# A third pair of F tiles by seven block products, with loads, block sums and the units' order moved to suit, in a SwiGLU kernel on one core

## The chip, the cores and the metric

The kernel runs on one core of one Trainium2 chip. The metric is the device time of one execution in microseconds (us); from several runs the median is given. Engines are named as in the profile: PE is TensorE, ACT ScalarE, DVE VectorE, POOL GpSimd, SP SyncE, which issues most transfers.

## The reference

```python
B, S, D, F = 1, 2048, 512, 1376          # all bfloat16
def reference(x, w_gate, w_up, w_down):
    g = jax.nn.silu(x @ w_gate)          # [2048, 1376]
    u = x @ w_up
    return (g * u) @ w_down              # [2048, 512]
```

## The kernel before

**Tiling.** The 2048 tokens are four chunks of 512 (`SC`); chunks 0 and 1 are the first half (`pi = 0`), 2 and 3 the second (`pi = 1`). F is ten tiles of 128 and a remainder of 96. The ten tiles form five pairs; pair `u` holds tiles `2u` and `2u+1`. `xT_sb` holds x transposed (D on the partitions), `w_sb` gate and up weights, `wd_sb` w_down. `h0_sb` and `h1_sb` hold h = silu(gate) * up for the two token halves.

**Two ways to make h.** A *classic* tile (F tile, chunk) is 4 matmuls for gate and 4 for up in bfloat16 (`gu_emit` at L410, each split in two column halves, or `gu_whole` at L421), then a silu on ACT and a product on DVE (`classic_out`). A *unit* (token half, pair) treats two F tiles x two chunks x two halves of D as a 2x2 block product and makes it with seven block products instead of eight, for gate and for up: `p1` and `p2` in bfloat16 (L605), and `p6`, `p5`, `p7`, `p3`, `p4` (L593) with 4-byte operands that are sums of blocks. A unit has 28 matmuls, four classic tiles have 32. The sums of weight blocks S1 to S4 and a cast A22 are made by `w_sums` in `ss_sb` (POOL, casts on ACT or POOL; four slots); the sums of token blocks T1 to T4 and a cast B22 by `x_sums` in `tt_sb` (DVE for the first half, POOL for the second). S2 reads S1, S4 reads S2; T2 reads T1, T4 reads T2. Products after p7 and p3 leave through adds on DVE (`sums`, into `ts_sb`), a silu on ACT and a product on POOL; those after p2 and p4 through a silu and a DVE product (`direct`). `p1` and `keep` copy partial sums aside on ACT and DVE.

`U_ORDER` says which pairs are units in which half: before, pairs 3 and 4 of the first half and all five of the second. The other tiles of the first half are classic.

**Order.** TensorE's order is the order in which the program calls these functions; SP's is that of the `load` calls. ACT, DVE and POOL get theirs from `Plan.schedule`, a list planner: it repeatedly takes the operation that could start first by its model (busy and lag of each operation, landing times of the loads), and among equal starts the one with the lower `prio`. `after` adds dependences. Planned times set only the order; at run time semaphores decide.

TensorE's order before: transposes of the first 256 tokens, classic tiles 0 and 1 of chunk 0, classic tiles 2 to 5 of chunk 0, classic tiles 0 to 2 of chunk 1, the remainder of F for all four chunks (`plan_x`, `plan_y`, L474 and L500, which need x2 and x3), p1 of the first unit, then the units. One classic tile of chunk 1 stands ahead of the first unit's p6, one between its p6 and p5, and one in the last unit ahead of p3. In each unit the order is p6, p5, p7, p2, p1 of the next unit, p3, p4. The weight sums of pair 0 are made first; DVE's `x_sums(0)` waits for them (`after`), the weight sums of the first half's pairs wait for `x_sums(0)`, and `x_sums(1)` on POOL waits for these.

After the units comes the down product (`down`): matmuls over h for half of the tokens' tiles, the remainder's (`tails`), and `DownUnit`, again with seven block products, whose sums DVE and POOL make (`down_sums`; T1 and T2 in `tt_sb`, T3 and T4 in `th_sb`, which lies over `w_sb`). POOL gets the h products of the units at priority 3, weight sums at 8.

SP's loads before: `xn` (first 256 tokens), gate and up weights of tiles 0-1 (`wg0`, `wu0`) with `x0b` between them, tiles 2-3 (`wg2`, `wu2`), tiles 4-5 (`wg4`, `wu4`), `x1`, tiles 6-7, tiles 8 and on, `wut`, `x2`, `x3`, then w_down. x beyond the first 256 tokens comes by transposing transfers.

Of the kernel before, what the change touches and what calls it, by code (L numbers as in the profile page):

```python
# [5 lines left out]
ALU = mybir.AluOpType  # L6
BF16 = mybir.dt.bfloat16
FP32 = mybir.dt.float32
# [6 lines left out]
A_BUSY, A_LAG = 485, 180  # L15
# [152 lines left out]
def bass_standalone__swiglu_ffn__prompt_kernel(nc, x, w_gate, w_up, w_down, out):  # L168
    _, S, D = x.shape
    F = w_gate.shape[1]  # L170
    P = 128
    KD = D // P
    KH = KD // 2
    NFF = F // P
    U_ORDER = [[3, 4], [0, 3, 4, 1, 2]]
    F_LAST = F - NFF * P
    SC = 512
    NSC = S // SC
# [13 lines left out]
    xf = x[0]  # L192
# [5 lines left out]
    with ExitStack() as es:  # L198
# [25 lines left out]
        ss_sb = sb("ss_sb", [P, NSLOT, 5, 2, KH, P], F32R)  # L224
        tt_sb = [tt0_sb, sb("tt1_sb", [P, 5, KH, SC], F32R)]
# [24 lines left out]
        plan = Plan()  # L250
        engines = {"P": nc.tensor, "S": nc.sync, "A": nc.scalar, "D": nc.vector, "G": nc.gpsimd}

        landed = 2700

        def load(name, emit, writes, busy, lag):
            nonlocal landed
            landed += lag
            i = take(homes[name] if name in homes else rest[0])
            plan.add("S", emit, writes=writes, busy=busy, lag=1800, dma=(i, 16)).land = landed + (2500 if landed > 10000 else 0)

        slabs = [(0, 2), (2, 4), (4, 6), (6, 8), (8, NFF + 1)]
        slab_of = {ft: a for a, b in slabs for ft in range(a, b)}

        def load_w(name, src, m, c0, f0, f1):
            load(
                name,
                lambda e: e.dma_start(  # L267
                    w_sb[:, :, m, c0:c0 + f1 - f0], src[:, f0:f1].rearrange("(k p) f -> p k f", p=P)
                ),
                [name], 600, 3.2 * (f1 - f0),  # L270
            )

        def load_slab(a, b):
            load_w(f"wg{a}", w_gate, 0, a * P, a * P, min(b * P, F))
            load_w(f"wu{a}", w_up, 1, a * P, a * P, min(b * P, F - 32))

        def load_x(name, t0, t1):
            load(
                name, lambda e: e.dma_start_transpose(xT_sb[:, :, t0:t1], xf[t0:t1, :]), [name], 1500, 4.6 * (t1 - t0)  # L279
            )  # L280

        load(
# [6 lines left out]
        load_w("wg0", w_gate, 0, 0, 0, slabs[0][1] * P)  # L289
        load_x("x0b", HT, SC)  # L290
        load_w("wu0", w_up, 1, 0, 0, slabs[0][1] * P)
        for a, b in slabs[1:3]:
            load_slab(a, b)
        load_x("x1", SC, 2 * SC)
        for a, b in slabs[3:]:
            load_slab(a, b)
        load_w("wut", w_up, 0, F, F - 32, F)
        for c in range(2, NSC):
            load_x(f"x{c}", c * SC, (c + 1) * SC)
        load(  # L300
            "wd",
            lambda e: e.dma_start(
# [31 lines left out]
        def tt_op(engs, out, a, b, alu, reads, writes, prio, busy, after=()):  # L334
            return plan.add(
                engs, lambda e: e.tensor_tensor(out, a, b, alu), reads, writes, busy,  # L336
                G_LAG if engs == "G" else D_LAG, prio, after=after,
            )
# [44 lines left out]
        for dk in range(KD):  # L383
            keys = [("b", 2 * dk), ("b", 2 * dk + 1)] if dk < KD - 1 else [("b", 6)]
# [136 lines left out]
        W_SUM = {"S1": 0, "S2": 1, "S3": 2, "S4": 3, "A22": 4}  # L521
        X_SUM = {"T1": 0, "T2": 1, "T3": 2, "B22": 3, "T4": 4}
        slot_of = {}

        def cast_op(eng, out, src, reads, writes, prio, busy, after):
            plan.add(
                eng, lambda e: e.activation(out, src, ACT.Copy) if eng == "A" else e.tensor_copy(out, src),
                reads, writes, busy, A_LAG if eng == "A" else G_LAG, prio, after=after,
            )

        def w_sums(u, prio, after, casts):

            f0, f1 = 2 * u * P, (2 * u + 1) * P
            slot = len(slot_of) % NSLOT
            slot_of[u] = slot
            block = lambda m, k, f: w_sb[:, k * KH:(k + 1) * KH, m, f:f + P]
            at = lambda n, m: ss_sb[:, slot, W_SUM[n], m, :, :]
            key = lambda n, m: ("ss", slot, n, m)
            wkey = lambda m: f"w{'gu'[m]}{slab_of[2 * u]}"
            for n in ("S1", "S2", "S3", "S4"):  # L540
                for m in range(2):
                    A11, A12, A21, A22 = (block(m, k, f) for f in (f0, f1) for k in range(2))
                    rd = lambda n: at(n, m).bitcast(FP32)
                    a, b, alu, of_ = {
                        "S1": (A21, A22, ALU.add, ()), "S2": (rd("S1"), A11, ALU.subtract, ["S1"]),
                        "S3": (A11, A21, ALU.subtract, ()), "S4": (A12, rd("S2"), ALU.subtract, ["S2"]),
                    }[n]
                    last = tt_op(
                        "G", at(n, m), a, b, alu, [wkey(m)] + [key(o, m) for o in of_], [key(n, m)], prio, 640, after
                    )  # L550
            for m in range(2):
                cast_op(casts, at("A22", m), block(m, 1, f1), [wkey(m)], [key("A22", m)], prio, 360, after if casts == "G" else ())
            return [last]

        def x_sums(pi, eng, prio, after):

            c0, c1 = 2 * pi, 2 * pi + 1
            xk = x_keys(c0) + x_keys(c1)
            key = lambda n, k: ("tt", pi, X_SUM[n], k)
            steps = [(0, KH)] if eng == "D" else [(k, k + 1) for k in range(KH)]  # L560
            for n in ("T1", "T2", "T3", "T4"):
                for k0, k1 in steps:
                    block = lambda k, c: xT_sb[:, k * KH + k0:k * KH + k1, c * SC:(c + 1) * SC]
                    at = lambda n: tt_sb[pi][:, X_SUM[n], k0:k1, :]
                    rd = lambda n: at(n).bitcast(FP32)
                    B11, B12, B21, B22 = (block(k, c) for k in range(2) for c in (c0, c1))
                    a, b, of_ = {
                        "T1": (B12, B11, ()), "T2": (B22, rd("T1"), ["T1"]),
                        "T3": (B22, B12, ()), "T4": (B21, rd("T2"), ["T2"]),
                    }[n]  # L570
                    last = tt_op(
                        eng, at(n), a, b, ALU.subtract, xk + [key(o, k) for o in of_ for k in range(k0, k1)],
                        [key(n, k) for k in range(k0, k1)], prio, 1150 if eng == "D" else 1250, after,
                    )
            for k in range(KH):
                cast_op("A", tt_sb[pi][:, X_SUM["B22"], k, :], xT_sb[:, KH + k, c1 * SC:(c1 + 1) * SC], xk, [key("B22", k)], prio, A_BUSY, ())
            return [last]

        class Unit:
            def __init__(self, pi, u, banks):  # L580
# [90 lines left out]
        wkey = [f"wg{slab_of[0]}", f"wu{slab_of[0]}"]  # L671
# [320 lines left out]
        units = [(pi, u) for pi in range(2) for u in U_ORDER[pi]]  # L992
        early = [2 * u + i for u in range(NFF // 2) if u not in U_ORDER[0] for i in range(2)]
        sums = w_sums(0, 8, (), "A")
        for fts in [[2, 3]] + [[ft] for ft in early[4:]]:
            classic(0, fts)
        for ft in early[:-3]:
            classic(1, [ft])
        sums = x_sums(0, "D", 6, sums)
        for u in U_ORDER[0]:  # L1000
            sums = w_sums(u, 8, sums, "A")
        sums = x_sums(1, "G", 8, sums)

        pool_last = []

# [67 lines left out]
```

## Time and profile before

| | |
|---|---|
| runs shown | 115.79, 116.16, 117.97 us; median 116.16 |
| profiled execution | 115.73 us, span 114.4 us, clock 1.00 |
| busy, share of the span | PE 96%, PEld 58%, DVE 67%, ACT 53%, POOL 52% |
| chain that ended last | PE 91%, DMA 3%, SP's queue 2% |
| seven-block matmuls of the units | 140, busy 35.3 us |
| units, up to the down product | 26.04 to 75.69 us |

Times in the profile run from the start of the span. The chain lists, back from the last instruction, what released each step; a stretch of it on one engine is a stretch in which only that engine's work set the end.

### The profile page before, as it was taken

Reading aid. Unit: us, or ns where it says so; the run is one execution under the profiler, and the core shown is the slowest. Engines: PE = TensorE matmul, PEld = TensorE weight load, DVE = VectorE, ACT = ScalarE, POOL = GpSimd, SP = SyncE. Lnnn points to the kernel's source line nnn. Section 1 sums busy time; section 2 is a strip of 40 time slices with the busy share of each in tenths; the row PEclk is TensorE's granted clock in tenths of the full one; section 3 lists DMA queues with packets and bytes.
Section 4 is the critical chain, followed back from the end, with each engine's and each line's share of the span. In section 5 each row is a group of like instructions: output and inputs, shape, how many; then the busy total and the mean of one; then the engine's idle time right before and its main releaser. Section 6 shows DMA issues by size and latency. Waiting matters only on the chain.

```text
span 114.4 us, 1807 instructions
## 1 busy us (share of the span) xinstructions
PE 110.3 (96%) x662; PEld 66.7 (58%) x670; DVE 76.3 (67%) x112; ACT 60.9 (53%) x116; POOL 59.9 (52%) x75
## 2 busy tenths in 40 slices
PE   7989999999999999999999999999999999999993
PEld 2645555554567667685858677554344657866452
DVE  0112599766659395776849393799999987486423
ACT  5344285599756767878676767630576960000000
POOL 1475000599999999799999999981000000000000
DMA  3999999993000000000000000000041002327966
GB/s 96 255 307 257 212 282 232 239 356 78 0 0 0 0 3 3 0 6 0 3 0 0 0 0 0 0 6 0 2 135 46 0 0 46 52 46 183 200 190 207
DMA packets 22776, 9.84 MB, mean 86 GB/s; under 512 B 12816, under 2 KB 22640, under 8 KB 22768
## 3 DMA queue, kind: packets, MB, share of 16 engines
q1 hardware_dynamic: 20624, 8.69, 31.1%
q10 hardware_dynamic: 2144, 1.05, 3.2%
q8 instruction: 5, 0.08, 0.3%
q14 instruction: 3, 0.02, 0.1%
HBM read 4.75 MB, written 2.10 MB: 60 GB/s over the span
## 4 chain that ended last, share of the span: by engine, by line
PE 91%; DMA 3%; SPq 2%; issue 1%; DVE 1%
PE psum L593 28%; PE psum L703 15%; PE psum L410 12%; PE psum L605 10%; PE psum L841 10%; PE psum L421 5%; PE psum L853 4%; DMA w_sb<-in_w_up_dram 3%; PE psum L474 3%; PE psum L731 3%; PE psum L500 2%; SPq L279 1%; DVE o_sb L325 1%; SPq L267 0%; SPq L284 0%
## 5 line engine op out<-in xcount | busy, mean ns | idle before, releaser
L593 PE MATMUL psum<-tt_sb,ss_sb 128*128 128x512 f32 x140 | 35.3, 404 | 0.0
L593 PEld LDWEIGHTS psum<-tt_sb,ss_sb 128*128 128x128 f32 x140 | 26.3, 188 | 6.4
L336 DVE TENSOR_TENSOR ts_sb<-r_sb,psum 128x512 f32<-128x512 f32 x28 | 17.9, 682 | 12.4 <-ACT r_sb L324 12.4
L336 DVE TENSOR_TENSOR h_sb<-sg_sb,psum 128x512 bf16<-128x512 f32 x26 | 17.8, 683 | 8.6 <-PE psum L410 7.0
L331 ACT ACTIVATE sg_sb<-psum 128x512 f32<-128x512 f32 x26 | 15.5, 598 | 14.5 <-PE psum L410 8.0
L336 POOL TENSOR_TENSOR ss_sb<-w_sb 128x256 fp32r<-128x256 bf16 x20 | 13.1, 677 | 15.1 <-DVE tt_sb L336 11.1
L336 POOL TENSOR_TENSOR h_sb<-sg_sb,ts_sb 128x512 bf16<-128x512 f32 x14 | 18.4, 1316 | 1.7 <-ACT sg_sb L331 1.5
L324 ACT ACTIVATE r_sb<-psum 128x512 f32<-128x512 f32 x28 | 15.2, 595 | 5.7 <-PE psum L593 5.7
L703 PE MATMUL psum<-wd_sb,h_sb 128*128 128x512 bf16 (+2 forms) x97 | 18.0, 335 | 0.2
L410 PE MATMUL psum<-xT_sb,w_sb 128*64 128x512 bf16 (+1 forms) x160 | 15.9, 358 | 0.7 <-DMA w_sb<-in_w_up_dram 0.5
L703 PEld LDWEIGHTS psum<-wd_sb,h_sb 128*128 128x128 bf16 x100 | 8.3, 98 | 9.2 <-issue 1.0
L410 PEld LDWEIGHTS psum<-xT_sb,w_sb 128*64 128x64 bf16 x160 | 8.8, 110 | 7.6 <-DMA w_sb<-in_w_up_dram 0.8
L605 PE MATMUL psum<-xT_sb,w_sb 128*128 128x512 bf16 x52 | 12.6, 380 | 0.4 <-issue 0.2
L331 ACT ACTIVATE sg_sb<-ts_sb 128x512 f32<-128x512 f32 x14 | 8.9, 633 | 1.6 <-DVE ts_sb L336 1.6
L605 PEld LDWEIGHTS psum<-xT_sb,w_sb 128*128 128x128 bf16 x56 | 4.8, 98 | 7.0 <-issue 2.3
L336 POOL TENSOR_TENSOR ss_sb<-w_sb,ss_sb 128x256 fp32r<-128x256 bf16 x10 | 6.6, 686 | 0.0
L336 POOL TENSOR_TENSOR ss_sb<-ss_sb,w_sb 128x256 fp32r<-128x256 f32 x10 | 6.6, 678 | 0.0
L325 DVE CAST o_sb<-psum 128x512 bf16<-128x512 f32 (+2 forms) x6 | 2.9, 512 | 4.2 <-PE psum L703 3.1
L421 PE MATMUL psum<-xT_sb,w_sb 128*128 128x512 bf16 x24 | 5.7, 379 | 0.0
L841 PE MATMUL psum<-tt_sb,ss_sb 128*128 128x512 f32 x20 | 5.7, 420 | 0.0
L324 ACT ACTIVATE o_sb<-psum 128x512 bf16<-128x512 f32 x4 | 2.3, 596 | 6.1 <-PE psum L731 5.1
L325 DVE COPY psum<-psum 128x512 f32<-128x512 f32 x7 | 4.9, 700 | 0.9 <-ACT sgy_sb L331 0.3
(71 smaller groups left out, 126.9 us busy)
## 6 DMA issues: line engine op xcount, KB each, us to landing
wd_sb<-in_w_down_dram SPq DMA_DIRECT2D x1, 1280.0 KB, 7.8
w_sb<-in_w_gate_dram SPq DMA_DIRECT2D x4, 256.0 KB, 4.1
w_sb<-in_w_up_dram SPq DMA_DIRECT2D x4, 256.0 KB, 4.3
out_dram<-o_sb SPq DMA_DIRECT2D x7, 128.0 KB, 1.8
out_dram<-xT_sb ACTq DMA_DIRECT2D x4, 128.0 KB, 2.4
out_dram<-xT_sb ACTq DMA_DIRECT2D x2, 256.0 KB, 3.3
w_sb<-in_w_gate_dram SPq DMA_DIRECT2D x1, 352.0 KB, 4.9
w_sb<-in_w_up_dram SPq DMA_DIRECT2D x1, 320.0 KB, 4.2
```

The costliest lines, as they stand in the source:

```text
L324: return e.activation(out, src, ACT.Copy)
L325: return e.tensor_copy(out, src)
L331: "A", lambda e: e.activation(out, src, ACT.Silu), reads, writes, busy, A_LAG, prio
L336: engs, lambda e: e.tensor_tensor(out, a, b, alu), reads, writes, busy,
L410: ins = e.matmul(psum[h:h + HC, b, n0:n1], lhsT=w_sb[:, dk, m, ft * P + h:ft * P + h + HC], rhs=xT_sb[:, dk, c * SC + n0:c * SC + n1], sta ...
L421: ins = e.matmul(bank(b), lhsT=w_sb[:, dk, m, ft * P:(ft + 1) * P], rhs=xT_sb[:, dk, c * SC:(c + 1) * SC], start=(dk == 0), stop=(dk == KD ...
L474: ins = e.matmul(psum[m:m + HC, b, :], lhsT=w_sb[:, dk, 0, XC0 + m:XC0 + m + HC], rhs=xT_sb[:, dk, c * SC:(c + 1) * SC], start=(dk == 0), ...
L593: ins = e.matmul(bank(dst), lhsT=s[:, k, :], rhs=t[:, k, :], start=(start and k == 0), stop=(k == KH - 1), skip_group_check=True,)
L605: ins = e.matmul(bank(dst), lhsT=w_sb[:, k0 + k, m, f:f + P], rhs=xT_sb[:, k0 + k, c:c + SC], start=(start and k == 0), stop=(k == KH - 1) ...
L703: ins = e.matmul(psum[:, b, 0:c1 - c0], lhsT=hrows(F_ORDER[n], t, 0, P), rhs=wd_sb[:, F_ORDER[n], c0:c1], start=(start and n == n0), stop= ...
L841: ins = e.matmul(bank(dst), lhsT=self.ds[s][:, j, self.q, :], rhs=self.dt[t][:, j, :], start=(start and n == 0), stop=(n == NFF // 2 - 1), ...
L853: ins = e.matmul(bank(dst), lhsT=wd_sb[:, 2 * j + a, d * P:(d + 1) * P], rhs=h0_sb[:, 2 * j + a, 0:SC], start=(n == 0), stop=(n == NFF // ...
```

## The change

1. `U_ORDER` becomes `[[2, 4, 3], [0, 2, 4, 3, 1]]`: pair 2 (tiles 4 and 5) of the first half is a unit too. Classic tiles 4 and 5 of chunks 0 and 1 are gone; so are the classic tiles between p6 and p5 of the first unit and in the last unit.
2. Load order: `x1` directly after tiles 2-3; tiles 6-7 after `x3`. The planner's landing times are set anew.
3. `w_sums` makes each sum for gate and up in one POOL instruction of 512 elements instead of two of 256, which waits for both weights; its A22 casts get priority 8.
4. `x_sums` chains each T after the one before it; its casts get priority 8. Priorities of the later weight sums and of `x_sums(1)` go from 8 to 2.
5. In the last unit p4 comes ahead of p3.

```diff
-    U_ORDER = [[3, 4], [0, 3, 4, 1, 2]]
+    U_ORDER = [[2, 4, 3], [0, 2, 4, 3, 1]]
...
-        for a, b in slabs[1:3]:
-            load_slab(a, b)
+        load_slab(*slabs[1])
         load_x("x1", SC, 2 * SC)
-        for a, b in slabs[3:]:
-            load_slab(a, b)
+        load_slab(*slabs[2])
+        load_slab(*slabs[4])
         load_w("wut", w_up, 0, F, F - 32, F)
         for c in range(2, NSC):
             load_x(f"x{c}", c * SC, (c + 1) * SC)
+        load_slab(*slabs[3])
...
+            block = lambda k, f: w_sb[:, k * KH:(k + 1) * KH, :, f:f + P].rearrange("p k m c -> p m k c")
+            at = lambda n: ss_sb[:, slot, W_SUM[n], :, :, :]
...
             for n in ("S1", "S2", "S3", "S4"):
-                for m in range(2):
...
-                        "G", at(n, m), a, b, alu, [wkey(m)] + [key(o, m) for o in of_], [key(n, m)], prio, 640, after
+                last = tt_op("G", at(n), a, b, alu, wkeys + [k for o in of_ for k in keys(o)], keys(n), prio, 1180, after)
...
+            last = after
             for n in ("T1", "T2", "T3", "T4"):
-                for k0, k1 in steps:
+                before = last
+                last = []
+                for k0, k1 in [(0, KH)] if pi == 0 else [(k, k + 1) for k in range(KH)]:
...
-                        [key(n, k) for k in range(k0, k1)], prio, 1150 if eng == "D" else 1250, after,
+                        [key(n, k) for k in range(k0, k1)], prio, 1160 if eng == "D" else 1250, before,
...
-        for fts in [[2, 3]] + [[ft] for ft in early[4:]]:
-            classic(0, fts)
-        for ft in early[:-3]:
+        classic(0, [2, 3])
+        for ft in early[:3]:
             classic(1, [ft])
         sums = x_sums(0, "D", 6, sums)
         for u in U_ORDER[0]:
-            sums = w_sums(u, 8, sums, "A")
-        sums = x_sums(1, "G", 8, sums)
+            sums = w_sums(u, 2, sums, "A")
+        sums = x_sums(1, "G", 2, sums)
...
-        classic(1, early[-3:-2], [6, 7])
+        classic(1, early[3:], [6, 7])
         for n in range(len(units)):
             unit.p6()
-            if n == 0:
-                classic(1, early[-2:-1], [2, 3])
             unit.p5()
             unit.p7()
             unit.p2()
             if n + 1 < len(units):
                 after = make(n + 1)
                 after.p1()
+                unit.p3()
+                unit.p4()
             else:
-                free = 2 * (1 - n % 2)
-                classic(1, early[-1:], [free, free + 1])
-            unit.p3()
-            unit.p4()
+                unit.p4()
+                unit.p3()
```

More of the change, by code (lines that the diff above doesn't have):

```diff
@@ L258, in load @@
             i = take(homes[name] if name in homes else rest[0])
-            plan.add("S", emit, writes=writes, busy=busy, lag=1800, dma=(i, 16)).land = landed + (2500 if landed > 10000 else 0)
+            plan.add("S", emit, writes=writes, busy=busy, lag=1800, dma=(i, 16)).land = landed + (0 if landed < 5000 else 500 if landed < 10000 else 500)
         slabs = [(0, 2), (2, 4), (4, 6), (6, 8), (8, NFF + 1)]
@@ L269, in load_w @@
                 ),
-                [name], 600, 3.2 * (f1 - f0),
+                [name], 600, 3.7 * (f1 - f0),
             )
@@ L278, in load_x @@
             load(
-                name, lambda e: e.dma_start_transpose(xT_sb[:, :, t0:t1], xf[t0:t1, :]), [name], 1500, 4.6 * (t1 - t0)
+                name, lambda e: e.dma_start_transpose(xT_sb[:, :, t0:t1], xf[t0:t1, :]), [name], 1500, 5.2 * (t1 - t0)
             )
@@ L535, in w_sums @@
             slot_of[u] = slot
[L536 to L539, printed above, removed]
+            block = lambda k, f: w_sb[:, k * KH:(k + 1) * KH, :, f:f + P].rearrange("p k m c -> p m k c")
+            at = lambda n: ss_sb[:, slot, W_SUM[n], :, :, :]
+            keys = lambda n: [("ss", slot, n, m) for m in range(2)]
+            wkeys = [f"w{g}{slab_of[2 * u]}" for g in "gu"]
             for n in ("S1", "S2", "S3", "S4"):
-                for m in range(2):
[L542 to L548, printed above, removed]
-                        "G", at(n, m), a, b, alu, [wkey(m)] + [key(o, m) for o in of_], [key(n, m)], prio, 640, after
-                    )
+                A11, A12, A21, A22 = (block(k, f) for f in (f0, f1) for k in range(2))
+                rd = lambda n: at(n).bitcast(FP32)
+                a, b, alu, of_ = {
+                    "S1": (A21, A22, ALU.add, ()), "S2": (rd("S1"), A11, ALU.subtract, ["S1"]),
+                    "S3": (A11, A21, ALU.subtract, ()), "S4": (A12, rd("S2"), ALU.subtract, ["S2"]),
+                }[n]
+                last = tt_op("G", at(n), a, b, alu, wkeys + [k for o in of_ for k in keys(o)], keys(n), prio, 1180, after)
             for m in range(2):
-                cast_op(casts, at("A22", m), block(m, 1, f1), [wkey(m)], [key("A22", m)], prio, 360, after if casts == "G" else ())
+                cast_op(
+                    casts, at("A22")[:, m], w_sb[:, KH:2 * KH, m, f1:f1 + P], [wkeys[m]], [("ss", slot, "A22", m)], 8, 360,
+                    after if casts == "G" else (),
+                )
             return [last]
@@ L559, in x_sums @@
             key = lambda n, k: ("tt", pi, X_SUM[n], k)
-            steps = [(0, KH)] if eng == "D" else [(k, k + 1) for k in range(KH)]
+            last = after
             for n in ("T1", "T2", "T3", "T4"):
-                for k0, k1 in steps:
+                before = last
+                last = []
+                for k0, k1 in [(0, KH)] if pi == 0 else [(k, k + 1) for k in range(KH)]:
                     block = lambda k, c: xT_sb[:, k * KH + k0:k * KH + k1, c * SC:(c + 1) * SC]
@@ L570, in x_sums @@
                     }[n]
-                    last = tt_op(
+                    last.append(tt_op(
                         eng, at(n), a, b, ALU.subtract, xk + [key(o, k) for o in of_ for k in range(k0, k1)],
-                        [key(n, k) for k in range(k0, k1)], prio, 1150 if eng == "D" else 1250, after,
-                    )
+                        [key(n, k) for k in range(k0, k1)], prio, 1160 if eng == "D" else 1250, before,
+                    ))
             for k in range(KH):
-                cast_op("A", tt_sb[pi][:, X_SUM["B22"], k, :], xT_sb[:, KH + k, c1 * SC:(c1 + 1) * SC], xk, [key("B22", k)], prio, A_BUSY, ())
-            return [last]
+                cast_op("A", tt_sb[pi][:, X_SUM["B22"], k, :], xT_sb[:, KH + k, c1 * SC:(c1 + 1) * SC], xk, [key("B22", k)], 8, A_BUSY, ())
+            return last
         class Unit:
```

## The prediction

> **What bounds the kernel now.** I read the page first (span, busy slices, chain), then the chain of waits in order of time, then the timelines of the engines that feed TensorE, and last the issues and landings of the loads.
>
> ```profile
> span 114.4 us, 1807 instructions
> ...
> PE   7989999999999999999999999999999999999993
> ...
> POOL 1475000599999999799999999981000000000000
> ...
> PE 91%; DMA 3%; SPq 2%; issue 1%; DVE 1%
> ...
> 35.01:75.69 40.68, 40.48 (x178) 28.44 (x181) 28.28 (x46) 28.98 (x56) 39.24 (x42) 1.00 0.01 1
> ```
>
> The last row is from the table of stages (stage, its length, then busy time of PE, PEld, DVE, ACT, POOL, then the granted clock). TensorE (PE) is 91% of the chain, and in the stage of the seven-block units (35.01 to 75.69) it is busy 40.48 of 40.68 us at clock 1.00: there is next to no hole to close. GpSimd (POOL) is busy 39.24 of the same 40.68 us. So time can be won only by taking matmuls away, and lost by making TensorE wait; the engine nearest to making it wait is GpSimd. The chain, piece by piece (start, length):
>
> ```profile
> 6.85 14.00 PE psum L410 x128
> ...
> 23.45 1.73 PE psum L474 x16
> ...
> 26.04 0.16 issue
> 26.20 0.81 PE psum L605 x3
> 27.01 1.73 PE psum L421 x8
> 28.73 0.92 PE psum L593 x4
> 29.65 1.74 PE psum L421 x8
> ...
> 35.01 4.66 PE psum L593 x20
> ...
> 41.41 4.61 PE psum L593 x20
> 46.02 1.74 PE psum L605 x8
> ...
> 72.10 1.73 PE psum L421 x8
> 73.83 1.86 PE psum L593 x8
> ```
>
> From 6.85 us TensorE runs on without a wait: 16 classic groups (14.00/16 = 0.875 us each), the tails (20.85 to 26.04; the row at 23.45 is the product of x2 and then that of x3), the first unit's p1, classic tiles at L421 (1.74 us for gate and up), and units of 20 four-byte matmuls (4.61) and 8 two-byte ones (1.74), 6.35 us a unit.
>
> **The change, part by part.**
>
> *Matmuls.* Pair 2 (F tiles 4 and 5) of chunks 0 and 1 leaves the classic path: four L410 groups, 4 x 0.875 = 3.50 us, and two L421 tiles, 1.73 + 1.74 = 3.47. A unit is added: 4.61 + 1.74 = 6.35. Net -0.62 us, all on the path. This is the whole possible gain: 0.5% of the time.
>
> *What the classic work covered.* 3.50 us of it stood before the tails, 1.74 between p6 and p5 of the first unit, 1.73 in the last unit. Whatever these hid now comes due earlier. The rest asks, for each, what is late next.
>
> *Loads.* The rows give the issue on SP (start, length), and for the loads the time from issue to landing.
>
> ```profile
> 4.20 0.51 SPq L267 DMA_DIRECT2D w_sb<-in_w_up_dram  x1
> 4.76 0.51 SPq L267 DMA_DIRECT2D w_sb<-in_w_gate_dram  x1
> 5.31 0.51 SPq L267 DMA_DIRECT2D w_sb<-in_w_up_dram  x1
> 5.86 4.21 SPq L279 DMA_TRANSPOSE xT_sb<-in_x_dram  x1
> w_sb<-in_w_up_dram SPq DMA_DIRECT2D x1, 256.0 KB, 4.4
> w_sb<-in_w_up_dram SPq DMA_DIRECT2D x1, 256.0 KB, 5.0
> xT_sb<-in_x_dram SPq DMA_TRANSPOSE x1, 7.7
> 17.07 2.49 SPq L279 DMA_TRANSPOSE xT_sb<-in_x_dram  x1
> xT_sb<-in_x_dram SPq DMA_TRANSPOSE x1, 4.5
> ```
>
> These are wu2, wg4, wu4, x1, then the landings of wu2 (4.20 + 4.4 = 8.6), wu4 (5.31 + 5.0 = 10.3), x1 (5.86 + 7.7 = 13.6), and x3 (17.07 + 4.5 = 21.6). x1 landed 3.3 us behind the load before it. Put behind wu2 it lands at 8.6 + 3.3 = 11.9; if only its issue moved (two issues, 1.1 us) it lands at 12.5. Classic chunk 1 needs it after six groups, 6.85 + 5.25 = 12.1 (before: after ten, 15.6). So 0 to 0.4 us of wait; I take 0. x2 and x3 move ahead of slab 6-7 (512 KB; two such loads took 10.3 - 8.6 = 1.7 us): x3 at about 19.9. TensorE reaches x3's tail product 3.50 us earlier than before; that product starts at 23.45 + 0.86 = 24.3 now, so at 20.8: slack 0.9 us; x2 is due 0.9 us earlier and lands 2 earlier. Slab 6-7 is now behind x3 and first used past 30 us. All covered, but with slack of 1 us where there were 2.7. The w_down loads stay behind all of these and are first used at 75 us.
>
> *Token sums T on VectorE (pi = 0).*
>
> ```profile
> 11.47 0.69 DVE L336 TENSOR_TENSOR h_sb<-sg_sb,psum 128x512 bf16<-128x512 f32 x1 [1.90 <-PE psum L410]
> 14.67 1.22 DVE L336 TENSOR_TENSOR tt_sb<-xT_sb 128x1024 fp32r<-128x1024 bf16 x1
> 19.87 1.22 DVE L336 TENSOR_TENSOR tt_sb<-xT_sb,tt_sb 128x1024 fp32r<-128x1024 bf16 x1
> 21.16 1.30 POOL L336 TENSOR_TENSOR ss_sb<-w_sb 128x256 fp32r<-128x256 bf16 x2 [11.09 <-DVE tt_sb L336]
> ```
>
> Four sums of 1.22 us with classic products (0.69) between them; GpSimd idled 11.09 us until the last was done (21.1). After the change T1 can start when x1 is there (11.9) and h of tile 2 is out (12.16). It also waits for the first weight sums: joined, these start only when wu0 has landed (6.85) and take four instructions, to about 11.6. So T1 at 12.2, and with three 0.69 us products between the sums T4 ends at 12.2 + 4 x 1.22 + 3 x 0.69 = 19.1: GpSimd starts 2 us earlier. The bound on the late side is 21.1, as now.
>
> *Joined weight sums.* No row shows the joined 512-element form. Nearest rows:
>
> ```profile
> 31.58 2.29 POOL L336 TENSOR_TENSOR tt_sb<-xT_sb 128x512 fp32r<-128x512 bf16 x2 [0.17 <-POOL ss_sb L336]
> ...
> 35.07 1.29 POOL L336 TENSOR_TENSOR h_sb<-sg_sb,ts_sb 128x512 bf16<-128x512 f32 x1
> ...
> 37.70 1.30 POOL L336 TENSOR_TENSOR h_sb<-sg_sb,ts_sb 128x512 bf16<-128x512 f32 x1 [0.20 <-ACT sg_sb L331]
> ...
> 66.31 1.44 POOL L336 TENSOR_TENSOR ss_sb<-wd_sb 128x640 fp32r<-128x640 bf16 x1
> ```
>
> Two halves one after the other take 1.26 to 1.30 (row at 21.16): the upper end, 1.30. A contiguous 512-element sum takes 2.29/2 = 1.15. A strided 640-element one takes 1.44, by elements 1.15 for 512. I take 1.15 (lower end 1.12). The order changes too: S2 needs S1, which is now the instruction just before, so the planner puts S3 between; each unit's sums then hold two waits of about 0.15 (0.17 in the row): 4 x 1.15 + 0.3 = 4.9 us, bounds 4.8 to 5.5 (5.1 in the separate form).
>
> *Where GpSimd meets TensorE.* TensorE after the change: tails at 17.35 to 22.5, p1 to 23.5, the last classic tile to 25.2, then p6 of unit 0 at 25.2, and 6.35 us a unit. S2 of the first pair is due at 25.2: 19.1 + 3 x 1.15 = 22.6, covered, and at 21.1 still 24.6. Unit 3, the first of tokens 1024-2047, needs its T2 at p6, 25.2 + 3 x 6.35 = 44.3, T3 at p7, 46.1, T4 at 49.7 (before, T2 was due at 43.3 and GpSimd had had two pairs' weight sums to do ahead of it; now three). GpSimd's queue up to the end of T3: three pairs, 3 x 4.9 = 14.7; T1, T2, T3, two of 1.15 each, 6.9; and h products of 1.25 us each (1.29 in the row, overlapping) that are let in at the waits. By priorities and the time each is ready (1.8 us after its p7 or p3: p3 of unit 0 ended at 35.01 + 0.92, its product began at 37.70) four come ahead of T3: 5.0. Sum 26.6, from 19.1: T3 at 45.7 against 46.1. T4 takes one more h product and 2.3 us: 49.3 against 49.7. No wait, by 0.4 us. The bounds: three h products and 1.12 us, 43.6, no wait; start at 21.1, 1.30 us a sum and five products, 21.1 + 16.5 + 7.2 + 6.3 = 51.1, a wait of 5.0. I take no wait, nearest to the worked order, but this is the narrowest place.
>
> *p5 of unit 0.* It used to follow a second classic tile. It writes the banks that the classic tile has just filled. Before, that tile ended at 28.73 and its product left VectorE so:
>
> ```profile
> 29.82 0.69 DVE L336 TENSOR_TENSOR h_sb<-sg_sb,psum 128x512 bf16<-128x512 f32 x1
> ```
>
> That is 1.78 us after the tile's end. Now p5's second half comes 0.92 + 0.46 = 1.38 us after it: a wait of 0.4 us, down to 0 if ScalarE's casts fall elsewhere (they get priority 8). I take 0.25.
>
> *End of the units.* p4 goes ahead of p3 and the 1.73 us classic tile is gone. p3 needs both adds of p7 done on VectorE; in every other unit p3 follows p7 by 1.74 us (the row at 46.02, p2 and the next p1) without a wait, and now by p2 and p4, 0.87 + 0.92. The last h product, on GpSimd, left at 76.03 + 1.52 = 77.55, 2.8 us after p3's end (73.83 + 0.93); the down stage runs 18 matmuls of 0.217 (3.9 us) before it needs it. Covered by 1.1 us.
>
> ```profile
> 75.74 0.68 DVE L336 TENSOR_TENSOR th_sb<-h_sb 128x512 fp32r<-128x512 bf16 x1
> 76.34 1.76 DVE L336 TENSOR_TENSOR tt_sb<-h_sb 128x512 fp32r<-128x512 bf16 x1
> 76.03 1.52 POOL L336 TENSOR_TENSOR h_sb<-sg_sb,ts_sb 128x512 bf16<-128x512 f32 x1 [0.34 <-ACT sg_sb L331]
> ```
>
> These rows speak against the edit: the same 512-element sum on VectorE took 0.68 alone and 1.76 beside a GpSimd product, and that product 1.52 instead of 1.29. With the classic tile gone, w_sb is free 1.73 us sooner relative to the units' end, so T3 and T4 of the down stage can start among the last unit's adds. One sum slowed by 1.76 - 0.68 = 1.1 us just eats the cover of 1.1; two leave a wait of 1.1. I take 0, upper bound 1.1. The Trainium skill, GPSIMD Engine Reference, 1. Specifications, says that GpSimd's memory interfaces are shared with VectorE, with contention when a VectorE instruction has two SBUF inputs; the trace agrees, by those 1.76 us against 0.68.
>
> *Sum.* The profiled execution took 115.73 us (span 114.4 and 1.3 around it). 115.73 - 0.62 + 0.25 = 115.4. Of the runs shown the lowest is 115.79 and the median 116.16, 0.4 above the profiled one; I forecast the median with half of that: **115.6 us**.
>
> **The rivals.**
>
> 1. *The gain is eaten* by one wait of 0.7 to 2 us: T of unit 3 (GpSimd starting at 20.5, or one h product more), or the end of the units. 115.6 + 1.2 = 116.8. For it: 0.4 us of slack in a sum of 26.6. Against it: each term has a row.
> 2. *The loads are late*: x1 at 12.5 (only the issue moved) and x3 about 0.3 late. 115.6 + 0.6 = 116.2. For it: the transposing issue held SP for 4.21 us. Against: landings followed the order of issue. A delay here also gives GpSimd room later.
> 3. *Slower, by T of unit 3.* Place: p6 and p7 of unit 3, TensorE waiting on GpSimd. If the T sums on VectorE end at 21.1 as now and the joined sum costs 1.30, with five products ahead: the bound above, a wait of 5.0, 115.6 + 5.0 = 120.6; with four products and 1.26 it is 3.0, 118.6. It is over 2% (118.5) when T3 ends past 49.0. For it: GpSimd is already 96% busy there and gets a third pair's sums, 4.9 us, ahead of T. Against: the 2 us earlier start.
> The Trainium skill, TensorE: Matmul & The Clock Gate, Part 1, says that an idle window of about 3.4 us halves the clock; every stage here shows 1.00, so no run shows it. By that rule a wait of 5 us would cost up to 3.4 us more, an estimate, and 124 instead of 120.6.
> 4. *Faster by over 2%* would need 2.3 us; the matmuls give 0.62 and there is no hole of TensorE to close after 6.85.
>
> **How the numbers follow.** Forecast 0.50, rival 1 0.29, rival 2 0.10, rival 3 0.10, rival 4 0.01. Two per cent, 2.3 us, is about what a measurement of this kernel can tell from no change. Faster 0.01; within 2%: 0.50 + 0.29 + 0.10 = 0.89; slower 0.10. The range: below, the sum without the 0.25 and with the median as low as the profiled run, 115.1, less 0.3 for spread, 114.8; above, rival 1 with its full 2 us, 117.6.
>
> **What would show it.** Right: 160 matmuls in the units' four-byte group, 8 in the whole classic group, 96 of 512 columns in the split classic group; 20 joined 128x512 weight sums near 1.15 us; the first GpSimd sum after its idle time near 19; no wait of PE on tt_sb. Wrong: a piece of the chain on POOL tt_sb ahead of L593 near 44 to 50 us (rivals 1 and 3); PE waiting on DMA xT_sb near 12 or 20 us (rival 2); GpSimd starting again at 21 or its joined sums at 1.3; PE waiting on h_sb behind the last unit.

## The result, and the profile after

The changed kernel takes 116.91 us (median of 17 runs) against 115.79 us before (17 runs): ratio 1.0101, 95% interval 1.0076 to 1.0127. The ratio leaves out three runs of the kernel before (117.69 to 117.97 us) that count as slow. The kernel is slower by 1%, where 115.6 us had been forecast, with a gain of about 0.4 us in its sum (-0.62 + 0.25). The profiled execution took 116.91 us, 1.18 more than that of before. First the page (rows of the page; below the chain come two groups of instructions with count, busy time, mean in ns, idle time before). Lines behind 570 have moved by two: L593 is L595 now, L605 is L607, L841 is L843, L853 is L855.

```profile
span 115.6 us, 1763 instructions
...
PE   7999999999999999999999999999999799999993
...
POOL 1069004999999999958999979144000000000000
...
PE 72%; DVE 15%; DMA 7%; SPq 3%; issue 1%
...
L595 PE MATMUL psum<-tt_sb,ss_sb 128*128 128x512 f32 x160 | 40.3, 404 | 0.0
...
L336 POOL TENSOR_TENSOR ss_sb<-w_sb 128x512 fp32r<-128x512 bf16 x10 | 11.4, 1157 | 13.5 <-DVE tt_sb L336 7.3
```

TensorE had 91% of the chain; now VectorE has 15% of it, and the PE row has a 7 in slice 31 (near 90 us), where there were nines. The chain of waits in order of time (start, length) shows three places:

```profile
4.75 7.56 DMA xT_sb<-in_x_dram
...
12.45 5.37 PE psum L410 x48
...
25.70 3.16 PE psum L595 x12
28.85 1.74 PE psum L607 x8
30.59 4.66 PE psum L595 x20
...
78.65 6.57 DVE tt_sb L336 x6
85.22 2.87 DVE th_sb L336 x3
...
90.70 0.61 DVE r_sb L336
...
91.36 1.43 PE psum L843 x5
```

1. x1 lands at 12.31 and TensorE starts chunk 1 at 12.45 instead of 12.1; its six groups take 5.37 instead of 5.25. Together 0.47 us.
2. p6, p5, p7 of the first unit take 3.16 us; the same 12 matmuls take 2.77 at 0.231 us each. 0.39 us. In the list of waits (total, times, longest) TensorE's weight loads (PEld) have two there, one in p6 for VectorE's copy of p1's result and one in p5 for the product of the classic tile whose bank it writes:

```profile
PEld psum L595 <- DVE psum L325: 0.4, 1, 0.4
...
PEld psum L595 <- DVE h_sb L336: 0.3, 1, 0.3
```

3. From 78.65 to 91.31 the chain is VectorE alone: it makes the sums for the down product. Behind them in its queue stands the add (`keep`) that must empty a bank before TensorE's next group of seven-block matmuls in the down stage (`DownUnit`) can start. In TensorE's timeline the units end at 73.74 + 2.21 = 75.95, and the wait is the idle time at 91.36:

```profile
73.74 2.21 PE L595 MATMUL psum<-tt_sb,ss_sb 128*128 128x512 f32 x8
...
91.36 1.43 PE L843 MATMUL psum<-tt_sb,ss_sb 128*128 128x512 f32 x5 [0.61 <-DVE r_sb L336]
```

From the end of the units to the end of the span it is 115.6 - 75.95 = 39.65 us, against 114.4 - 75.69 = 38.71 before. 0.94 us, of which the wait itself is 0.61; most of the rest is that the five matmuls behind it take 1.43 us instead of 1.16.

With the matmuls taken away, -0.62 + 0.47 + 0.39 + 0.94 = +1.18 us: the whole difference of the two profiles. The unit itself is not dearer than forecast by more than 0.05 us: in the chain its 8 and 20 matmuls take 1.74 + 4.66 = 6.40 us, where 6.35 had been put in, and the four classic groups and two tiles that it replaces took 6.97. GpSimd, which the prediction called the narrowest place, made TensorE wait nowhere. Its timeline:

```profile
18.84 2.27 POOL L336 TENSOR_TENSOR ss_sb<-w_sb 128x512 fp32r<-128x512 bf16 x2 [7.29 <-DVE tt_sb L336]
...
31.78 1.29 POOL L336 TENSOR_TENSOR h_sb<-sg_sb,ts_sb 128x512 bf16<-128x512 f32 x1
...
42.43 2.28 POOL L336 TENSOR_TENSOR tt_sb<-xT_sb 128x512 fp32r<-128x512 bf16 x2
```

It starts again at 18.84 and has T3 at 44.7; unit 3 uses it at 47.1.

VectorE and GpSimd around the end of the units (their timelines):

```profile
73.42 1.29 DVE L336 TENSOR_TENSOR ts_sb<-r_sb,psum 128x512 f32<-128x512 f32 x2 [1.83 <-ACT r_sb L324]
...
75.22 1.63 DVE L336 TENSOR_TENSOR th_sb<-h_sb 128x512 fp32r<-128x512 bf16 x1
...
78.57 3.78 DVE L336 TENSOR_TENSOR tt_sb<-h_sb 128x512 fp32r<-128x512 bf16 x3
82.27 2.95 DVE L336 TENSOR_TENSOR tt_sb<-h_sb,tt_sb 128x512 fp32r<-128x512 bf16 x3
...
90.62 0.68 DVE L336 TENSOR_TENSOR r_sb<-psum,ts_sb 128x512 f32<-128x512 f32 x1
```

```profile
75.03 1.28 POOL L336 TENSOR_TENSOR h_sb<-sg_sb,ts_sb 128x512 bf16<-128x512 f32 x1 [2.39 <-ACT sg_sb L331]
78.26 1.27 POOL L336 TENSOR_TENSOR h_sb<-sg_sb,ts_sb 128x512 bf16<-128x512 f32 x1 [1.95 <-ACT sg_sb L331]
```

Two stretches of T sums are slow (1.63 for one of 0.68; 3.78 for three that take 2.96 elsewhere), each beside a GpSimd product. Before, one was (1.76 us). And before, the same add left VectorE 0.6 us ahead of its use:

```profile
71.44 1.28 DVE L336 TENSOR_TENSOR ts_sb<-r_sb,psum 128x512 f32<-128x512 f32 x2 [1.83 <-ACT r_sb L324]
...
73.94 0.69 DVE L336 TENSOR_TENSOR h_sb<-sg_sb,psum 128x512 bf16<-128x512 f32 x1 [0.62 <-PE psum L421]
...
80.89 2.95 DVE L336 TENSOR_TENSOR tt_sb<-h_sb,tt_sb 128x512 fp32r<-128x512 bf16 x3
...
89.24 0.68 DVE L336 TENSOR_TENSOR r_sb<-psum,ts_sb 128x512 f32<-128x512 f32 x1
```

It ended at 89.92, and TensorE's product that waits for it began at 90.49: 0.57 us of slack.

Counted from the units' end (75.69 before, 75.95 after), the add starts 13.55 us behind it before and 14.67 after: 1.12 us later, twice the slack. The rows say where the 1.12 come from. VectorE's last stretch of work, from the adds of the last p7 on (71.44 before, 73.42 after), starts 1.72 us later against the units' end, which is the classic tile that is gone. Of that, 1.22 are taken up, by the idle 0.62 us ahead of the classic tile's product and by the 0.60 of that product. The second slow stretch adds the 0.6 that are left. The delay stands at 1.12 us by the sums at 80.89 (before) and 82.27 (after), and is 1.12 still at the add.

### The profile page after: what moved, and what is told of

It reads as the page before. It is cut to its first block, busy times and chain, and to the rows that moved or that the text cites. A ratio compares the mean times of both kernels' runs of the same rounds, so it can differ in the third digit from the quotient of the medians.

```text
span 115.6 us, 1763 instructions
## 1 busy us (share of the span) xinstructions
PE 111.7 (97%) x650; PEld 69.0 (60%) x650; DVE 78.7 (68%) x115; ACT 63.8 (55%) x123; POOL 58.5 (51%) x55
## 3 DMA queue, kind: packets, MB, share of 16 engines
HBM read 4.75 MB, written 2.10 MB: 59 GB/s over the span
## 4 chain that ended last, share of the span: by engine, by line
PE 72%; DVE 15%; DMA 7%; SPq 3%; issue 1%
PE psum L595 31%; PE psum L607 12%; PE psum L843 9%; DMA xT_sb<-in_x_dram 7%; PE psum L705 6%; DVE tt_sb L336 6%; PE psum L410 5%; DVE th_sb L336 4%; PE psum L474 3%; PE psum L855 3%; SPq L267 2%; PE psum L421 1%; PE psum L500 1%; DVE ss_sb L336 1%; SPq L279 1%
## 5 line engine op out<-in xcount | busy, mean ns | idle before, releaser
L595 PE MATMUL psum<-tt_sb,ss_sb 128*128 128x512 f32 x160 | 40.3, 404 | 0.0
L595 PEld LDWEIGHTS psum<-tt_sb,ss_sb 128*128 128x128 f32 x160 | 29.9, 188 | 7.8 <-DVE psum L325 0.4
L336 DVE TENSOR_TENSOR ts_sb<-r_sb,psum 128x512 f32<-128x512 f32 x32 | 20.5, 681 | 15.0 <-ACT r_sb L324 15.0
L336 POOL TENSOR_TENSOR ss_sb<-w_sb 128x512 fp32r<-128x512 bf16 x10 | 11.4, 1157 | 13.5 <-DVE tt_sb L336 7.3
L607 PE MATMUL psum<-xT_sb,w_sb 128*128 128x512 bf16 x64 | 15.4, 381 | 0.0
L410 PE MATMUL psum<-xT_sb,w_sb 128*64 128x512 bf16 (+1 forms) x128 | 12.8, 353 | 0.5 <-DMA xT_sb<-in_x_dram 0.3
L607 PEld LDWEIGHTS psum<-xT_sb,w_sb 128*128 128x128 bf16 x64 | 5.5, 98 | 8.0 <-issue 2.5
L843 PE MATMUL psum<-tt_sb,ss_sb 128*128 128x512 f32 x20 | 5.6, 417 | 0.6 <-DVE r_sb L336 0.6
L336 POOL TENSOR_TENSOR ss_sb<-w_sb,ss_sb 128x512 fp32r<-128x512 bf16 x5 | 5.8, 1169 | 0.2
L336 POOL TENSOR_TENSOR ss_sb<-ss_sb,w_sb 128x512 fp32r<-128x512 f32 x5 | 5.8, 1161 | 0.0
L843 PE MATMUL psum<-th_sb,ss_sb 128*128 128x512 f32 x20 | 5.5, 413 | 0.0
L855 PE MATMUL psum<-h_sb,wd_sb 128*128 128x512 bf16 x20 | 5.0, 381 | 0.0
```

Source lines behind the costliest of these rows:

```text
L410: ins = e.matmul(psum[h:h + HC, b, n0:n1], lhsT=w_sb[:, dk, m, ft * P + h:ft * P + h + HC], rhs=xT_sb[:, dk, c * SC + n0:c * SC + n1], sta ...
L595: ins = e.matmul(bank(dst), lhsT=s[:, k, :], rhs=t[:, k, :], start=(start and k == 0), stop=(k == KH - 1), skip_group_check=True,)
L607: ins = e.matmul(bank(dst), lhsT=w_sb[:, k0 + k, m, f:f + P], rhs=xT_sb[:, k0 + k, c:c + SC], start=(start and k == 0), stop=(k == KH - 1) ...
L843: ins = e.matmul(bank(dst), lhsT=self.ds[s][:, j, self.q, :], rhs=self.dt[t][:, j, :], start=(start and n == 0), stop=(n == NFF // 2 - 1), ...
L855: ins = e.matmul(bank(dst), lhsT=wd_sb[:, 2 * j + a, d * P:(d + 1) * P], rhs=h0_sb[:, 2 * j + a, 0:SC], start=(n == 0), stop=(n == NFF // ...
```

## The experiments

The theory that they start from: three waits of TensorE ate the gain, the largest because VectorE's sums for the down product lost their cover. The rivals: GpSimd is the bound; the unit itself is dearer than four classic tiles (the 6.40 us above speak against that). All ratios are to the kernel before, which ran beside each, with 95% intervals; the changed kernel has 1.0101. Differences between two runs are differences of their ratios (0.01 is 1.16 us) and are known to some 0.3 to 0.6 us. No run takes back the new order of the T sums and the new priorities (part 4 of the change) alone.

**T4 behind the first add.** The sums T4 and S4 of the down product are put behind the add in VectorE's order.

```diff
-            t_sum("T4")
-            s_sum("S4", "D", [t_ops["T4"]])
+            def late(after):
+                free["T4"] = free["T4"] + after
+                t_sum("T4")
+                s_sum("S4", "D", [t_ops["T4"]])
...
-            a.p1()
+            late([a.p1()])
             a.p5()
```

> The changed kernel, but the T4 and S4 sums of the down product stand behind the first add of the down product (keep) in VectorE's planned order; the same work is done. Theory: of the 1.2 us that the changed kernel lost, 0.97 us is TensorE waiting ahead of the second seven-block product of the down stage for that add, which VectorE reaches late (90.6 us) behind 1.9 us of T4 sums not needed until 98. Then the add leaves at about 89, the gap of TensorE at 90.6 to 91.4 closes, and the time falls by 0.8 to 1.0 us, to about 116.0. Rival: the loss lies in the units and the loads alone, and VectorE's lateness is covered: the time stays within 0.2 us of the changed kernel.

116.14 us, ratio 1.0021 (0.9993 to 1.0048). VectorE's timeline and the chain:

```profile
89.43 0.68 DVE L336 TENSOR_TENSOR r_sb<-psum,ts_sb 128x512 f32<-128x512 f32 x1
90.15 2.96 DVE L336 TENSOR_TENSOR th_sb<-h_sb,tt_sb 128x512 fp32r<-128x512 bf16 x3
```

```profile
90.52 0.66 PE psum L705 x3
91.18 1.16 PE psum L845 x5
```

The add now comes before the T4 sums, and the down product follows the piece before it without a gap; from the end of the units (76.38) to the end of the span (115.1) it is 38.7 us again. Same work, other order: the third wait is shown, and with it most of the loss.

**The first unit's banks and copy.** The last classic tile's up product goes to a bank that p5 doesn't write, and VectorE copies p1's result ahead of the remainder's product.

```diff
...
-        y_out(1, 3)
         unit = make(0)
-        unit.p1()
-        classic(1, early[3:], [6, 7])
+        y_out(1, 3, [unit.p1()])
+        classic(1, early[3:], [6, 2])
```

> The changed kernel, but the last classic tile writes its up product into a bank that the first unit's p5 does not write, and VectorE copies p1's result before it makes the remainder's product. Theory: the first unit's p6, p5, p7 took 3.16 us instead of 2.77 because p6 waited for the copy and p5 for the bank; the 0.39 us go, and with them 0.3 to 0.4 us of the time, unless the wait at the down stage takes some of it back (VectorE's sums there start after the units' end, which moves with TensorE). Rival: the 0.39 us are the cost of four-byte matmuls at that point and stay; no difference.

116.36 us, ratio 1.0041 (1.0016 to 1.0065). Its chain:

```profile
25.18 2.79 PE psum L595 x12
```

2.79 instead of 3.16 us: the second wait is shown, though not how it divides between p6 and p5, since both edits are in one run. The ratio fell by 0.7 us, more than 0.37; in this profile x1 landed at 11.8 and TensorE did not wait for it either.

**Loads in the order of before.**

```diff
         load_slab(*slabs[1])
-        load_x("x1", SC, 2 * SC)
         load_slab(*slabs[2])
+        load_x("x1", SC, 2 * SC)
+        load_slab(*slabs[3])
         load_slab(*slabs[4])
...
-        load_slab(*slabs[3])
```

> The changed kernel with the loads in the order of before: x1 behind tiles 4-5, tiles 6-7 ahead of x2 and x3. Theory: x1 sets the start of chunk 1's classic tiles; it landed at 13.56 in the kernel before, so TensorE waits 1.2 us longer than the 0.36 us of the changed kernel, and everything behind shifts: +1.1 to +1.3 us. GpSimd starts 1.2 us later too, with 2.4 us of slack at unit 3, so no wait is added there. Rival: GpSimd is the bound, and its later start adds a wait at unit 3 as well: over +2 us.

118.76 us, ratio 1.0227 (1.0181 to 1.0272): 1.5 us more than the changed kernel, by the intervals 0.9 to 2.1, where 1.1 to 1.3 were expected. Between the two profiles it is 1.9 us. The waits of TensorE in its profile (total, times, longest):

```profile
PE psum L410 <- DMA xT_sb<-in_x_dram: 1.5, 1, 1.5
...
PE psum L595 <- DVE psum L325: 0.5, 1, 0.5
```

x1 landed at 13.70, and chunk 1 started at 13.84 instead of 12.45: 1.39 of the 1.9. The other 0.5 is the second wait grown: the planner, given other landings, puts two casts of token blocks instead of one ahead of the remainder's last silus on ScalarE, the silus start 1.91 us later (25.03 instead of 23.12), and p6 waits longer for the copy of p1's result behind them. No wait for T at unit 3 appears. So the load order is worth keeping.

**p3 first in the last unit**, as before, without the classic tile.

```diff
             else:
-                unit.p4()
                 unit.p3()
+                unit.p4()
```

> The changed kernel, but the last unit keeps the order p3, p4 of before. Theory: with p4 first, the adds behind p3 and the first T sums meet GpSimd's last two products, and two T sums are slowed (1.63 and about 1.4 us instead of 0.68); with p3 first one is. VectorE reaches the down stage's first add about 0.5 us earlier, TensorE loses 0.1 to 0.2 us at p3 to the banks: -0.3 us, at most -0.5. Rival: the order makes no difference, since the classic tile that stood there and not the order gave the cover: 0.

116.39 us, ratio 1.0054 (1.0029 to 1.0079). VectorE's timeline and two pieces of the chain:

```profile
76.41 0.69 DVE L336 TENSOR_TENSOR tt_sb<-h_sb 128x512 fp32r<-128x512 bf16 x1
...
77.61 3.08 DVE L336 TENSOR_TENSOR tt_sb<-h_sb 128x1024 fp32r<-128x1024 bf16 x2
```

```profile
74.13 2.24 PE psum L595 x8
...
91.19 1.15 PE psum L843 x5
```

One stretch is slow (3.08 for two that took 2.35 in the kernel before) instead of two, the add is in time, and TensorE pays 2.24 - 1.86 = 0.38 us at p3 for it. About half a microsecond better in all: the swapped order belongs to the loss. The rival, that the order makes no difference, falls.

**The last two products on VectorE.** Is it GpSimd that makes those sums slow?

```diff
-            tt_op("G", hview(ft, c), sg, v, ALU.mult, [ksg, kv], [("h", ft, c)], 3, 1250, h_free(ft, c))
+            last = (self.pi, self.u) == units[-1]
+            tt_op("D" if last else "G", hview(ft, c), sg, v, ALU.mult, ..., 3, 0 if last else 1250, h_free(ft, c))
```

> The changed kernel, but VectorE makes the last unit's two h products that GpSimd made; the order of the rest on VectorE is the same. Theory: VectorE's two slow T sums (1.63, and 1.4 of the three that took 3.78, instead of 0.68) are slow because GpSimd runs a product at the same time. Without them VectorE gains 1.8 us and pays two products of 0.60: it reaches the down stage's first add 0.4 to 0.65 us earlier, and the time falls by as much. Rival: the slow sums have another cause (the wait for the tile, their operands); then VectorE gets 1.2 us more work and the time rises by up to 1.2 us.

116.25 us, ratio 1.0036 (1.0023 to 1.0049): 0.7 us less, with 1.2 us more work on VectorE.

```profile
75.99 0.69 DVE L336 TENSOR_TENSOR th_sb<-h_sb 128x512 fp32r<-128x512 bf16 x1
...
78.99 2.96 DVE L336 TENSOR_TENSOR tt_sb<-h_sb 128x512 fp32r<-128x512 bf16 x3
```

The sums that took 1.63 and 3.78 take 0.69 and 2.96, and with no hole on VectorE the add left at 90.91, just as TensorE came to need it (90.92). They were slow because of GpSimd.

**Filler in place of the classic tile.** Eight unused matmuls between the units and the down product; all other engines keep their order.

```diff
...
+        pe(fill, ["wd", ("h", 0, 0)], [("b", 0)], 0)     # 8 matmuls 128x512
         down(*down_sums(pool_last))
```

> The changed kernel, with eight matmuls of 128x512 that nothing uses (1.74 us, what the dropped classic tile took) between the last unit and the down product; the orders of VectorE, GpSimd and ScalarE are those of the changed kernel. Theory: the classic tile covered VectorE's sums for the down product; with as much cover again TensorE finds the first add done, the gap of 0.97 us closes, and the time rises by 1.74 - 0.97 = 0.8 us only. Rival: the gap is not a matter of cover, since VectorE moves with TensorE: the whole 1.74 us show.

117.63 us, ratio 1.0172 (1.0122 to 1.0222): +0.8 us (0.2 to 1.5), not 1.74. The chain:

```profile
75.90 1.74 PE psum L1040 x8
...
91.76 0.66 PE psum L705 x3
92.42 1.16 PE psum L843 x5
```

With 1.74 us of other work there the gap is gone (91.76 + 0.66 = 92.42). The dropped classic tile had been cover for VectorE's sums.

**Weight sums apart again**, gate and up in two instructions of 256 elements; the rest as changed.

```diff
...
-                last = tt_op("G", at(n), a, b, alu, wkeys + [...], keys(n), prio, 1180, after)
+                for m in range(2):
+                    ...
+                    last = tt_op("G", at(n, m), a, b, alu, [wkey(m)] + [...], [key(n, m)], prio, 640, after)
```

> The changed kernel, but the weight sums are made as before, gate and up in two instructions of 256 elements. Theory: GpSimd is not on the path; its third T sum ended 2.4 us ahead of its use at unit 3. With 5.1 us a pair instead of 4.8 it ends about 1 us later and still in time: no change, within 0.2 us. Rival: GpSimd is the bound that ate the gain, and 0.3 us a pair over three pairs show: +0.6 us or more, with TensorE waiting for T at unit 3.

119.40 us, ratio 1.0308 (1.0289 to 1.0327): +2.4 us, and the theory was wrong here. GpSimd's and VectorE's timelines, and TensorE's waits:

```profile
34.59 1.28 POOL L336 TENSOR_TENSOR h_sb<-sg_sb,ts_sb 128x512 bf16<-128x512 f32 x1
```

```profile
39.22 0.69 DVE L336 TENSOR_TENSOR h_sb<-sg_sb,psum 128x512 bf16<-128x512 f32 x1 [0.41 <-ACT sg_sb L331]
39.82 0.68 DVE L336 TENSOR_TENSOR ts_sb<-r_sb,psum 128x512 f32<-128x512 f32 x1
```

```profile
PE psum L600 <- DVE ts_sb L336: 1.2, 4, 0.4
```

T came in time, but the first h product ran at 34.6, behind all three pairs, instead of 31.8, and each later one was late as well. The four `ts_sb` tiles hold the sums of one unit's two products, two each: an add whose tile is still held is put behind another product in VectorE's order, and the bank that it would empty is what the second half of p3 or of the next p5 writes (four waits, 0.4 us the longest; the four matmuls behind each take 1.21 us instead of 0.92, which makes up the 2.4). Two differences were left to tell apart: the longer work, or the place of the products.

**Apart, but the products in their places.** The third pair's S4 waits for the first product.

```diff
...
-                        "G", at(n, m), a, b, alu, [wkey(m)] + [...], [key(n, m)], prio, 640, after
+                        "G", at(n, m), a, b, alu, [wkey(m)] + [...], [key(n, m)], prio, 640,
+                        [*after, *hold] if n == "S4" else after,
...
+            product = unit.p7()
+            if n == 0:
+                sums = w_sums(U_ORDER[0][2], 2, sums, "A", [product])
+                sums = x_sums(1, "G", 2, sums)
```

> As the run with the weight sums in two instructions each, but the third pair's S4 has to wait for the first unit's first h product, so that the h products stand on GpSimd ahead of it, as in the changed kernel, and VectorE's order is that of the changed kernel. Theory: the 2.5 us that the separate sums cost were not their 0.3 us a pair, but the place of the h products: without the wait that S4 has in the joined form the first product ran at 34.6 instead of 31.8, behind all three pairs, each later one came late too, and the adds that need its ts_sb tile held TensorE's p3 in three units. Then the time comes back to within 0.6 us of the changed kernel. Rival: it is GpSimd's longer work (0.3 us a pair, about 1 us up to T): then most of the 2.5 us stays.

117.65 us, ratio 1.0165 (1.0128 to 1.0201). Of 2.4 us, 1.7 came back: the place of the products was the larger part. The other 0.7, just above the 0.6 allowed, is the longer work, at the place that the prediction feared (GpSimd's and TensorE's timelines):

```profile
44.97 2.30 POOL L336 TENSOR_TENSOR tt_sb<-xT_sb 128x512 fp32r<-128x512 bf16 x2
```

```profile
47.42 1.17 PE L600 MATMUL psum<-tt_sb,ss_sb 128*128 128x512 f32 x4 [0.66 <-POOL tt_sb L336]
```

**Both repairs, and x1 in halves.** The first two edits together; then also x1 in two loads of 256 tokens, with gate and up of the first half ahead of the second.

```diff
-        load_x("x1", SC, 2 * SC)
+        load_x("x1", SC, SC + HT)
+        load_x("x1b", SC + HT, 2 * SC)
...
+            if c == 1 and fts == [0]:
+                for t0, t1, keys in ((0, HT, ["x1"]), (HT, SC, ["x1b"])):
+                    for m, b in ((0, gates[0]), (1, ups[0])):
+                        pe(gu_emit(m, 0, c, b, range(KD), t0, t1), keys + [...], [("b", b)], 2)
...
```

> The edits of the first two runs together: T4 behind the down stage's first add, and the last classic tile's up product in another bank with the copy ahead of the remainder's product. Theory: the two waits of TensorE, 0.97 and 0.39 us, are independent and both on the path, so the time falls by 1.2 to 1.4 us against the changed kernel, and what is left against the kernel before is the gain of the matmuls (-0.62) less the wait for x1 (0.4): -0.2 us, ratio 0.997 to 0.999. Rival: closing one wait opens another of the same size behind it, and the time stays near that of the better of the two single edits, ratio 1.002 or more.

115.56 us, ratio 0.9982 (0.9962 to 1.0002): 1.4 us less than the changed kernel, as expected: closing one wait does not open another.

> As the run with both edits, and x1 loaded in two halves of 256 tokens; the first classic tile of chunk 1 makes gate and up of the first half while the second half lands. Theory: TensorE's wait for x1 near 12 us (0.3 to 0.4 us in the profiles, from run to run 0 to 0.45) is covered by 0.88 us of matmuls: another -0.3 us, ratio to the kernel before 0.994 to 0.996. Rival: two transposing loads cost more than one on the queue (the second half lands later than the whole did), and the wait moves to the second half: no gain, or x2 and x3 late as well.

115.29 us, ratio 0.9960 (0.9940 to 0.9979): faster than both kernels. Its interval overlaps that of the run before it, so that x1's halves bring 0.25 us is not shown by the times; its chain shows the wait gone:

```profile
4.44 13.19 PE psum L412 x144
17.63 1.73 PE psum L481 x16
```

TensorE runs through x1's landing, and from 0.77 us to the last matmul the chain is TensorE.

## Why the prediction was right or wrong

The measured 116.91 lies in the range, and near the 116.8 of the first rival, which named "the end of the units" as one of its places and had 0.29. That its number is so near is luck: it has one wait of 1.2 us, and the trace has three, of 0.47, 0.39 and 0.94. The forecast itself had the wrong sign. Its 115.6 also held 0.2 us for a median above the profiled run; with 17 runs the median of before was 115.79, only 0.06 above it.

- *Matmuls, -0.62.* Right to 0.05 (the unit takes 6.40, not 6.35). With the three waits closed the kernel is 0.2 to 0.7 us faster than before.
- *Loads.* x1 landed at 12.31, between the 11.9 that I took and the 12.5 of the other bound; taken as 0, it cost 0.47. In the nine profiles of this load order with x1 in one piece it landed between 10.8 and 12.7. An early landing did not help by itself: in the run with p3 first, where x1 landed at 10.8, the up weights of tiles 0-1 held TensorE until 7.23, against 6.85 in the kernel before. The tails, forecast for 17.35, began between 17.30 and 18.25 in the nine, so a value above 0 should have stood in the sum.
- *T sums, joined sums, unit 3.* Right: start 18.84 (19.1), 1.157 us a sum (1.15), four products ahead of T3, T3 at 44.7 (45.7), used at 47.1 (46.1), no wait. Rival 3 fell with it. (The early bound for T3 adds up to 43.9, not 43.6, which changes nothing.) But the slack was said to hang on the sums' durations; the separate form shows that it hangs as much on the waits that let h products in.
- *p5 of the first unit.* 0.39 against 0.25 taken and a bound of 0.4. The size is nearly right, but partly by luck: part of it is p6, which waits for VectorE's copy, and the prediction had a price for p5 only.
- *End of the units.* The step that failed. The mechanism was named (VectorE's sums start among the last adds and two are slowed by GpSimd, "upper bound 1.1"), and the filler, the swapped order and the products on VectorE each confirm a part of it. But I followed it to one victim, the last h product, found it covered by 1.1 us, and took 0; measured, the term is 0.94. TensorE's matmuls did not wait for h_sb, the sign that the prediction gave for this place, but for r_sb. What was late was the thing in VectorE's queue with less cover: the add in the down stage, 13.55 us behind the units' end, which had 0.57 us (89.92 to 90.49) in the trace of before. VectorE was busy all the 11.81 us from the units' end to the first seven-block product of the down stage; a row of the stage table of before, which the prediction did not use, says so:

```profile
75.69:87.50 11.81, 11.71 (x84) 4.76 (x85) 11.81 (x14) 5.00 (x11) 1.53 (x2) 1.00 0.10 33
```

With no hole in VectorE's work there, nothing could take the delay up on the way: 1.12 us at 80.89 and 82.27, 1.12 at the add. That row asked for the 1.7 us of lost cover to be weighed against the slack at its far end.

## What to carry to other kernels

When work that TensorE did in between is removed, ask for every engine, not for the nearest consumer only, where its queue next meets TensorE, and measure the slack there; a row of a stage in which that engine is busy all the time says that the delay arrives undiminished, as it did here. Take cover away from a queue only after putting what is needed last at its end: moving the T4 sums behind one add gave back 0.9 us for the same work. And a shorter or joined instruction can matter more by the waits it makes, and by what is let in there, than by its length.

## What the runs showed of the hardware that I had not expected

- A VectorE sum with both inputs in SBUF of 512 elements took 0.68 us alone and 1.63 to 1.76 beside a GpSimd product of 512 elements. The sum seems to stand still until the product is over rather than to run slower: after, the product ended at 76.31 (75.03 + 1.28) and the sum at 76.85 (75.22 + 1.63), 0.54 behind; before, at 77.55 (76.03 + 1.52) and 78.10 (76.34 + 1.76), 0.55 behind, though the sum had started further into the product. The products lost little: 1.27 and 1.28 us, as elsewhere, and 1.52 once, when another such sum was running on VectorE as it began. With the products moved to VectorE the same sum took 0.69. The Trainium skill, GPSIMD Engine Reference, 1. Specifications, names the contention; the size is from these runs.
- The same transposing load of x1, issued at 4.75 us behind the same loads, landed 6.0 to 8.0 us later in nine profiles (6.0 in the run with p3 first, 7.99 in the run with T4 behind the first add). What moves it is not shown, nor how much of the kernels' spread in time comes from it.
